# Fewer v transfers, a shorter weight conversion and a zero-padded v operand in a windowed-attention and FFN kernel

## The chip, the cores and the metric

The kernel runs on one core of a Trainium2 chip. The metric is the device time of one execution in microseconds. Five engines work side by side, each through its own list of instructions in order: PE multiplies matrices (its weight loads are shown as PEld), DVE (VectorE) and ACT (ScalarE) work element by element, POOL (GpSimd) does fills and some elementwise work, and SP issues the transfers between main memory (HBM) and on-chip memory (SBUF). PE writes its results to PSUM, from where DVE and ACT read them.

## The reference

Attention over a causal window of 64 positions for 8 batches of 8 heads (576 positions, head dimension 64), and a two-layer FFN with softplus on the result (4608 tokens, 512 to 2048 to 512):

```python
scores = scale * np.matmul(q, k.transpose(0, 1, 3, 2))
mask = (rel >= 0) & (rel < 64)
scores = np.where(mask, scores, -1000000000.0)
scores = scores - np.max(scores, axis=-1, keepdims=True)
attn = np.exp(scores)
attn = attn / (np.sum(attn, axis=-1, keepdims=True) + 1e-09)
attn_out = np.matmul(attn, v).astype(np.float32)
x = attn_out.transpose(0, 2, 1, 3).reshape(B * S, H * D)
h = x @ w_in
g = np.maximum(h, 0.0) + np.log1p(np.exp(-np.abs(h)))
out = (g @ w_out).astype(np.float32)
```

q, k and v are float32, the two weight matrices float64.

## The kernel before, in words

The 4608 tokens are cut into 12 blocks of 384 (three tiles of 128). A block is worked on by head pairs: four pairs `hp`, each of two heads `hh`. The result of a pair is a tile x of 128 rows (features) by 384 tokens; four of them make the x of a block. In the profile's names x_3_0 is pair 3 of the first block, x_3_1 pair 3 of the second. x is kept as a high and a low part in a reduced f32 format, and so are the weights, so that each FFN product is made of three passes (high by high, high by low, low by high).

**FFN.** `ffn_up(g, f)` takes block g and slice f of 16 of the hidden layer: twelve passes on PE into `ps_h` (L403), three ACT steps and two DVE steps for the softplus and the split of g. `ffn_down(g, f)` is nine passes on PE into three banks `ps_o` (L424) that stay open over all slices. The first block is run for slices 0 to 7, the second for all 16, then the first for 8 to 15, then the other ten blocks.

**Weights.** They lie in HBM as float64 bits. `load_w(f)` loads slice f of both matrices (`raws`; later slices in two halves, `raw`) and makes float32 of it from the two 32-bit words of each number: ACT takes the absolute value of the high word read as a float32 (L167), four DVE steps put exponent, sign and mantissa together (L168 to L171), then ACT copies out the high part (L174) and POOL subtracts for the low part (L175). There are 20 such tiles: 12 with both matrices (`ws`, 1024 elements a row) and 8 with one (`wh`, 512).

**Attention of the first two blocks** (`by_pe`). q and k are used as they are: one product per tile into PSUM (L255), DVE adds the mask and finds the extreme of each row (L266), ACT takes the exponential (L276), DVE normalizes (L281 to L284), PE transposes (L291), and L349 multiplies with v in f32. For that product v lies in `v_pad` in two layouts that are shifted by 64 rows. Each head has 128 columns there, its own 64 and 64 zeros, so that both heads of a pair sum into one PSUM tile of 128 rows. The zeros come from two DVE memsets at the start (L121); the loads go tile by tile, nine for a pair (L226, L230).

**Attention of the other ten blocks.** q and k are split into a high and a low part (L237 to L244) and multiplied at L259. The normalized scores P and v are split in three bf16 parts. P goes through two transposing transfers (`nat` to `tr`); `v12` holds parts 1 and 2 of v side by side, so 128 columns of weights for a head, and `v13` holds part 3 of v in its lower half of rows and part 1 in its upper half, 64 columns for a head. The result is summed over up to seven pieces of the window with v12 (PSUM rows 0 to 127) and as many with v13 (PSUM rows 0 to 63), all at L378; then the two halves of the PSUM tile are added (L383, L384).

**Order.** The program makes a list of events with due times (`CONVERT`, `BASE`, `PACE`, `STG0` and so on) and emits them by due time. For events due before 100 (`PE_ORDERED_FROM`) the framework's scheduler sets the order of all engines from its own estimates of durations, so an edit moves instructions that it does not touch. From 100 on PE keeps the order in which the program emits, and the scheduler orders the others. SP has one queue for all transfers and issues them in its list's order; a transfer whose buffer is not free holds those behind it.

Of the kernel before, what the change touches and what calls it, by code (L numbers as in the profile page):

```python
# [20 lines left out]
CH = 64  # L21
NCH = TB // CH + 1
# [9 lines left out]
PE_ORDERED_FROM = 100  # L32
MANUAL = {mybir.EngineType.PE}

ZERO_HIGH = 2.0**-15


@with_exitstack
def window_attention_softplus_ffn(
# [24 lines left out]
    nc = tc.nc  # L64
# [44 lines left out]

    kbd_s = [att.tile([P, 2, CH + TB], F32, name="kbd", tag=f"k{i}") for i in range(2)]
    for t in kbd_s:
        nc.gpsimd.memset(t[D:P, 0, :], 0.0)
        nc.gpsimd.memset(t[0:D, 1, :], 0.0)
        nc.gpsimd.memset(t[0:D, 0, 0:CH], 0.0)
        nc.gpsimd.memset(t[D:P, 1, 0:CH], 0.0)
    v_pads = [att.tile([P, 2, NJ, 2, P], F32, name="v_pad", tag=n) for n in ("nat", "tr")]
    for t in v_pads:  # L120
        nc.vector.memset(t, 0.0)  # L121

# [18 lines left out]
    mask_b = cpool.tile([P, W], BF16, name="mask_b")  # L141
    nc.gpsimd.tensor_copy(mask_b, mask)
    nc.gpsimd.memset(mask_b[CH:P, 0:P], FAR)

    mm, tp = nc.tensor.matmul, nc.tensor.transpose

    def load_w(f):


        if f < NE + 4:  # L150
            k = (0, 4, 2, 6)[f % 4] if f < NE else (4, 6)[f % 2]
            parts = [(spare(k, [P, 2, DM], w_words.dtype, "raws"), spare(k + 1, [P, 2, DM], F32, "ws"), 0, 2)]
        else:
            parts = [
                (
                    ff.tile([P, 1, DM], w_words.dtype, name="raw"),
                    att.tile([P, 1, DM], F32, name="wh", tag=("v_in", "v12")[m]),
                    m, m + 1,
                )
                for m in range(2)  # L160
            ]
        for raw, w, m0, m1 in parts:
            nc.sync.dma_start(raw, w_words[f][:, m0:m1, :])
            words = raw.bitcast(U32).rearrange("p m (n two) -> p two m n", two=2)
            low, high = words[:, 0, :, :], words[:, 1, :, :]
            wb = w.bitcast(U32)
            nc.scalar.activation(w, high.bitcast(F32), AF.Abs)  # L167
            nc.vector.tensor_scalar(w, w, ZERO_HIGH, None, ALU.max)  # L168
            nc.vector.tensor_scalar(wb, wb, 3, 0x3FFFFFF8, ALU.logical_shift_left, ALU.bitwise_and)  # L169
            nc.vector.scalar_tensor_tensor(wb, high, 0xC0000000, wb, ALU.bitwise_and, ALU.bitwise_or)  # L170
            nc.vector.scalar_tensor_tensor(wb, low, 29, wb, ALU.logical_shift_right, ALU.bitwise_or)  # L171
# [9 lines left out]
    def attention(g, hp):  # L181
        c0 = hp * P
        t0 = ORDER[g] * TB
# [11 lines left out]
        heads = [slice(0, D), slice(D, P)]  # L195
# [20 lines left out]
        yield  # L216

        if by_pe:
            v_pad = v_pads[hp % 2]

            def load_v(rows, lay, j0, start):
                n = rows.stop - rows.start
                for j in range(j0, NJ):
                    dst = v_pad[rows, lay, j, :, :].rearrange("p h (i d) -> p (h i) d", i=2)[:, 0:4:3, :]
                    s = start + j * P
                    nc.sync.dma_start(dst, v[s : s + n, c0 : c0 + P].rearrange("p (h d) -> p h d", h=2))  # L226

            if t0 == 0:
                dst = v_pad[CH:P, 0, 0, :, :].rearrange("p h (i d) -> p (h i) d", i=2)[:, 0:4:3, :]
                nc.sync.dma_start(dst, v[0:CH, c0 : c0 + P].rearrange("p (h d) -> p h d", h=2))  # L230
            load_v(slice(0, P), 0, 1 if t0 == 0 else 0, t0 - CH)
            load_v(slice(0, CH), 1, 0, t0 + CH)
            load_v(slice(CH, P), 1, 0, t0)
# [16 lines left out]
        for j in range(NJ):  # L250
# [5 lines left out]
            else:  # L256
                for hh in range(2):
                    for i, part in enumerate((k_hi, k_lo)):
                        mm(  # L259
                            spv[:, hh, :], q_hl[:, hh, js], part[:, hh, kc],  # L260
                            start=(hh == 0 and i == 0), stop=(hh == 1 and i == 1), skip_group_check=True,
                        )
            t = ORDER[g] * NJ + j
# [9 lines left out]
        for hh in range(2):  # L273
            for j in range(NJ):
                i = hh * NJ + j
# [9 lines left out]
        if by_pe:  # L285

            pt = att.tile([P, 2, TB], F32, name="pt", tag="q_hl")
# [5 lines left out]
        else:  # L293

            nat = att.tile([P, 2, 4 * NJ, 2, CH], BF16, name="nat")
            tr = att.tile([P, 8 * NJ, P], BF16, name="tr")
# [5 lines left out]
            n = 4 * NJ  # L302
# [17 lines left out]
            yield  # L320

            v12 = att.tile([P, NCH, 2, 2, D], BF16, name="v12")
            v13 = att.tile([P, NCH, 2, D], BF16, name="v13")
            vv = v_in.rearrange("p c (h d) -> p c h d", h=2)
            up, low = heads
            nc.scalar.copy(v12[:, :, :, 0, :], vv)  # L326
            nc.vector.tensor_tensor(vv, vv, v12[:, :, :, 0, :], ALU.subtract)  # L327
            yield
            nc.scalar.copy(v12[:, :, :, 1, :], vv)
            nc.vector.tensor_tensor(v13[low, :, :, :], vv[low, :, :, :], v12[low, :, :, 1, :], ALU.subtract)  # L330
            nc.vector.tensor_copy(v13[up, :, :, :], v12[up, :, :, 0, :])
        yield

        if hp == 0:
# [5 lines left out]
        if by_pe:  # L340
            av = bank()
# [3 lines left out]
        for hh in range(2):  # L345
            if by_pe:
                for a in range(2 * NJ):
                    cs = slice(a * CH, (a + 1) * CH)
                    mm(  # L349
                        av[:, cs], v_pad[:, a % 2, a // 2, hh, :], pt[:, hh, cs],  # L350
                        start=(hh == 0 and a == 0), stop=(hh == 1 and a == 2 * NJ - 1), skip_group_check=True,
                    )
                if hh == 1:
                    nc.scalar.copy(x_t[0], av[:, :TB])
                    nc.vector.tensor_tensor(x_t[1], av[:, :TB], x_t[0].bitcast(F32), ALU.subtract)
                yield
                continue
            av = bank()
            passes = []
            for s in range(2):  # L360
                for c in range(0 if prev else 1, NCH):


                    j = (c - 1) // 2
                    n = s * 4 * NJ + (hh * NJ + j) * 2
# [10 lines left out]
                    passes.append((s, c, src, slice(o, o + (CH if c in (0, NCH - 1) else P))))  # L376
            for i, (s, c, src, osl) in enumerate(passes):
                mm(  # L378
                    av[: D if s else P, osl], v13[:, c, hh, :] if s else v12[:, c, hh, :, :], src,
                    start=(i == 0), stop=(i == len(passes) - 1), skip_group_check=True,  # L380
                )
            ds = heads[hh]
# [142 lines left out]
```

## Time and profile before

| | |
|---|---|
| three runs | 1057.53, 1059.34 and 1063.11 us, median 1059.34 |
| the profiled execution | 1059.67 us, of it span 1057.9 us |
| mean granted PE clock | 0.977 |
| busy in the span | PE 1004.5, PEld 883.0, DVE 813.9, ACT 740.2, POOL 54.4 us |
| DMA | 119.06 MB, mean 113 GB/s |
| L403 (up), L424 (down), PE busy | 448.9 and 436.4 us |
| L378, L259, L349, PE busy | 78.8, 78.8 and 25.8 us |

Busy time of PE is the union of its instructions, whose ends are modelled; how dense PE really is, is read from the distance between the starts of neighbouring instructions. A share of busy time is a mean over stages, so it is read by stretch. In the timeline a row merges neighbouring instructions of one line and shows the shape of the first; in the rows of groups the figures are the count, then busy us and mean ns of one, then idle us of the engine before them and who ended that.

### The profile page before, as it was taken

The numbers are of one execution on the slowest core, as the hardware profiler recorded it, in microseconds if no ns is written. First come the engines' busy times: TensorE is split into PE (matmuls) and PEld (weight loads), VectorE is DVE, ScalarE is ACT, GpSimd is POOL, SyncE is SP. The second block draws the span as 40 slices with busy tenths as digits, with TensorE's granted clock in tenths as the row PEclk, the third lists the DMA queues.
The fourth block names the chain that finished last, engine by engine and source line by source line (L and its number), as shares of the span: only waits on it lengthen the run. The fifth ranks groups of instructions, "written<-read, shape, count | busy, mean of one in ns | idle before, by whom it ended". The sixth has DMA issues, their size and how long they took to land.

```text
span 1057.9 us, 16725 instructions
## 1 busy us (share of the span) xinstructions
PE 1004.5 (95%) x5888; PEld 883.0 (83%) x5888; DVE 813.9 (77%) x1797; ACT 740.2 (70%) x1705; POOL 54.4 (5%) x53
## 2 busy tenths in 40 slices
PE   5768589999989999999999999999999999999998
PEld 3657488888778988888888888888888888888997
DVE  7889989667986778878877877877887887875322
ACT  4566479677776678778868877877877877865443
POOL 3233420000000000000000000000000000000000
PEclk8989769999999999999999999999999999999999
DMA  6576246344653436635534534534544554631000
GB/s 199 164 260 192 71 137 154 86 128 92 155 116 80 110 80 113 158 80 111 159 81 110 156 84 110 145 95 101 144 105 94 144 112 85 145 57 30 30 1 30
DMA packets 209748, 119.06 MB, mean 113 GB/s; under 512 B 143360, under 2 KB 201728, under 8 KB 208128
## 3 DMA queue, kind: packets, MB, share of 16 engines
q1 hardware_dynamic: 209664, 118.00, 45.0%
q8 instruction: 46, 0.75, 0.3%
q14 instruction: 38, 0.31, 0.1%
HBM read 76.28 MB, written 10.22 MB: 82 GB/s over the span
## 4 chain that ended last, share of the span: by engine, by line
PE 83%; DVE 10%; DMA 4%; ACT 1%; issue 1%; SPq 1%; ACTq 0%
PE ps_h L403 35%; PE ps_o L424 35%; PE ps_a L378 6%; PE ps_a L259 6%; DVE st L266 1%; DMA raws<-in_w_words_dram 1%; DVE ws L171 1%; DVE ws L170 1%; DVE st L284 1%; DMA v_in<-in_v_dram 1%; DVE ws L169 1%; DMA tr<-nat 1%; DMA kbd<-in_kT_dram 1%; DMA raw<-in_w_words_dram 1%; DVE ws L168 1%
## 5 line engine op out<-in xcount | busy, mean ns | idle before, releaser
L403 PE MATMUL ps_h<-x,w 128*128 128x384 f32 x2304 | 448.9, 342 | 9.4 <-DVE u L411 8.3
L424 PE MATMUL ps_o<-w,g 128*128 128x512 f32 x1728 | 436.4, 395 | 2.1 <-ACT g L413 2.1
L403 PEld LDWEIGHTS ps_h<-x,w 128*128 128x128 f32 x2304 | 406.8, 190 | 25.6 <-DVE u L411 11.0
L424 PEld LDWEIGHTS ps_o<-w,g 128*128 128x128 f32 x1728 | 319.2, 189 | 60.9 <-ACT g L413 2.7
L407 ACT ACTIVATE u<-ps_h 128x384 f32<-128x384 f32 x192 | 93.9, 489 | 135.3 <-PE ps_h L403 128.5
L411 DVE SCALAR_TENSOR_TENSOR u<-ps_h,u 128x384 f32<-128x384 f32 x192 | 106.2, 554 | 76.5 <-ACT u L409 75.3
L276 ACT ACTIVATE st<-st,mn 128x128 f32<-128x128 f32 x288 | 112.0, 390 | 17.7 <-DVE st L272 17.7
L414 DVE TENSOR_TENSOR g<-u,g 128x384 fp32r<-128x384 f32 x192 | 106.9, 558 | 12.0 <-ACT g L413 10.6
L266 DVE CUSTOM_DVE_ANT_0 st<-ps_a,mask 128x192 f32<-128x192 f32 x216 | 69.7, 352 | 58.5 <-PE ps_a L259 57.1
L408 ACT ACTIVATE u<-u 128x384 f32<-128x384 f32 x192 | 100.7, 526 | 3.3
L409 ACT ACTIVATE u<-u 128x384 f32<-128x384 f32 x192 | 100.3, 522 | 3.8
L378 PEld LDWEIGHTS <-v 128*128 128x128 bf16 (+1 forms) x1088 | 60.3, 104 | 30.8 <-issue 23.3
L378 PE MATMUL ps_a<-tr,v 128*64 128x128 bf16 (+3 forms) x1088 | 78.8, 215 | 3.3 <-DMA tr<-nat 3.3
L259 PE MATMUL ps_a<-k,q_hl 128*128 128x192 f32 x480 | 78.8, 288 | 0.0
L259 PEld LDWEIGHTS ps_a<-k,q_hl 128*128 128x128 f32 x480 | 67.2, 193 | 7.6
L413 ACT CAST g<-u 128x384 fp32r<-128x384 f32 x112 | 57.0, 509 | 21.6 <-DVE u L411 21.2
L307 ACT CAST nat<-st 128x768 bf16<-128x768 f32 x40 | 33.2, 831 | 38.3 <-DVE st L305 38.2
L383 ACT COPY xf<-ps_a 64x384 f32<-64x384 f32 x80 | 38.1, 476 | 25.6 <-PE ps_a L378 24.4
L276 ACT ACTIVATION_READ_ACCUMULATOR st<-st,mn 128x1 f32 x288 | 54.0, 188 | 0.0
L284 DVE TENSOR_TENSOR st<-st,sm 128x768 f32<-128x768 f32 x48 | 50.4, 1049 | 1.2
L384 DVE TENSOR_TENSOR xf<-ps_a,xf 64x384 f32<-64x384 f32 x80 | 43.8, 548 | 6.1 <-ACT xf L383 4.8
L327 DVE TENSOR_TENSOR v_in<-v_in,v 128x896 f32<-128x896 f32 x40 | 43.5, 1087 | 4.5 <-ACT v L326 4.5
(81 smaller groups left out, 885.7 us busy)
## 6 DMA issues: line engine op xcount, KB each, us to landing
k_in<-in_kT_dram SPq DMA_DIRECT2D x80, 224.0 KB, 3.8
v_in<-in_v_dram SPq DMA_DIRECT2D x80, 224.0 KB, 3.6
q_in<-in_qT_dram SPq DMA_DIRECT2D x84, 192.0 KB, 4.0
raws<-in_w_words_dram SPq DMA_DIRECT2D x12, 1024.0 KB, 5.7
out_dram<-raw SPq DMA_DIRECT2D x12, 512.0 KB, 2.8
raw<-in_w_words_dram SPq DMA_DIRECT2D x8, 512.0 KB, 5.3
out_dram<-raw SPq DMA_DIRECT2D x12, 256.0 KB, 2.6
v_pad<-in_v_dram SPq DMA_DIRECT2D x52, 32.0 KB, 2.7
```

The costliest lines, as they stand in the source:

```text
L259: mm(spv[:, hh, :], q_hl[:, hh, js], part[:, hh, kc], start=(hh == 0 and i == 0), stop=(hh == 1 and i == 1), skip_group_check=True,)
L266: nc.vector.tensor_tensor_reduce(st[:, hh, j, :], spv[:, hh, :], m, QSCALE, 3.0e38, ALU.add, ALU.min, mn[:, hh, j : j + 1])
L276: nc.scalar.activation(sv[:, i, 0:P], sv[:, i, 0:P], AF.Exp, bias=mn[:, hh, j : j + 1], scale=-1.0, accum_out=sm[:, i : i + 1])
L284: nc.vector.tensor_tensor(pn, pn, sm.unsqueeze(2).to_broadcast([P, 2 * NJ, P]), ALU.mult)
L378: mm(av[: D if s else P, osl], v13[:, c, hh, :] if s else v12[:, c, hh, :, :], src, start=(i == 0), stop=(i == len(passes) - 1), skip_grou ...
L403: mm(hv, weight(0, a, f)[:, c * P : (c + 1) * P], x[b][c], start=(i_mm == 0), stop=(i_mm == 3 * NC - 1))
L407: nc.scalar.activation(u, hv, AF.Abs)
L408: nc.scalar.activation(u, u, AF.Exp, scale=-1.0)
L409: nc.scalar.activation(u, u, AF.Ln, bias=1.0)
L411: nc.vector.scalar_tensor_tensor(gf, hv, 0.0, u, ALU.max, ALU.add)
L414: nc.vector.tensor_tensor(gt[1], gf, gt[0].bitcast(F32), ALU.subtract)
L424: mm(ops[g][j], gt[a][:, js], weight(1, b, f), start=(first and i == 0), stop=(last and i == 2),)
```

## The change

Three edits.

1. `v_pad` with its zeros is gone. `v_t` holds the pair's 128 columns without padding, and L347 writes each head's result into its own half of the PSUM rows with 64 columns of weights. All tiles of a layout come in one transfer: four loads for a pair of the first block, three for the second. Only a piece of 64 by 128 of each `v_t` is zeroed, by POOL.
2. The weights' ACT step scales by 2 to the power of -112, so that the exponent is right after the shift by 3 bits. The step that raised small values (L168) is gone; the sign step takes one bit in place of two.
3. `v13` becomes one tile for the whole program with 64 zero columns beside each head's 64, zeroed once by POOL. Its passes use 128 columns of weights and write all 128 PSUM rows.

```diff
-ZERO_HIGH = 2.0**-15
+REBIAS = 2.0**-112
...
-    v_pads = [att.tile([P, 2, NJ, 2, P], F32, name="v_pad", tag=n) for n in ("nat", "tr")]
-    for t in v_pads:
-        nc.vector.memset(t, 0.0)
+    v13 = cpool.tile([P, NCH, 2, 2, D], BF16, name="v13")
+    v_ts = [att.tile([P, 2, NJ, P], F32, name="v_t", tag=n) for n in ("nat", "tr")]
+    for t in v_ts:
+        nc.gpsimd.memset(t[0:CH, 0, 0, :], 0.0)
...
+    nc.gpsimd.memset(v13, 0.0)
...
-            nc.scalar.activation(w, high.bitcast(F32), AF.Abs)
-            nc.vector.tensor_scalar(w, w, ZERO_HIGH, None, ALU.max)
-            nc.vector.tensor_scalar(wb, wb, 3, 0x3FFFFFF8, ALU.logical_shift_left, ALU.bitwise_and)
-            nc.vector.scalar_tensor_tensor(wb, high, 0xC0000000, wb, ALU.bitwise_and, ALU.bitwise_or)
+            nc.scalar.activation(w, high.bitcast(F32), AF.Abs, scale=REBIAS)
+            nc.vector.tensor_scalar(wb, wb, 3, None, ALU.logical_shift_left)
+            nc.vector.scalar_tensor_tensor(wb, high, 0x80000000, wb, ALU.bitwise_and, ALU.bitwise_or)
             nc.vector.scalar_tensor_tensor(wb, low, 29, wb, ALU.logical_shift_right, ALU.bitwise_or)
...
-            def load_v(rows, lay, j0, start):
+            def load_v(rows, lay, j0, j1, start):
                 n = rows.stop - rows.start
-                for j in range(j0, NJ):
-                    dst = v_pad[rows, lay, j, :, :].rearrange("p h (i d) -> p (h i) d", i=2)[:, 0:4:3, :]
-                    s = start + j * P
-                    nc.sync.dma_start(dst, v[s : s + n, c0 : c0 + P].rearrange("p (h d) -> p h d", h=2))
+                src = v[start + j0 * P : start + j1 * P, c0 : c0 + P].rearrange("(j p) n -> p j n", p=P)
+                nc.sync.dma_start(v_t[rows, lay, j0:j1, :], src[:n, :, :])
...
-            nc.vector.tensor_tensor(v13[low, :, :, :], vv[low, :, :, :], v12[low, :, :, 1, :], ALU.subtract)
-            nc.vector.tensor_copy(v13[up, :, :, :], v12[up, :, :, 0, :])
+            nc.vector.tensor_tensor(v13[low, :, :, 0, :], vv[low, :, :, :], v12[low, :, :, 1, :], ALU.subtract)
+            nc.vector.tensor_copy(v13[up, :, :, 0, :], v12[up, :, :, 0, :])
...
-                        av[:, cs], v_pad[:, a % 2, a // 2, hh, :], pt[:, hh, cs],
-                        start=(hh == 0 and a == 0), stop=(hh == 1 and a == 2 * NJ - 1), skip_group_check=True,
+                        av[heads[hh], cs], v_t[:, a % 2, a // 2, heads[hh]], pt[:, hh, cs],
+                        start=(a == 0), stop=(a == 2 * NJ - 1), skip_group_check=True,
...
-                    av[: D if s else P, osl], v13[:, c, hh, :] if s else v12[:, c, hh, :, :], src,
+                    av[:, osl], (v13 if s else v12)[:, c, hh, :, :], src,
```

The new listing is two lines shorter: L403 is now L401, L424 is L422, L378 is L376, L349 is L347, L259 is L258, L291 is L290, and the DVE steps of the conversion are L171 to L173.

What the scheduler makes of it at three places. First SP, from behind the first pair's q and k: the loads of the first block. Before:

```order
3 L163 DMA raws<-in_w_words_dram 128x1024
4 L230 DMA v_pad<-in_v_dram 64x2x64
5 L226 DMA v_pad<-in_v_dram 128x2x64 x2
6 L226 DMA v_pad<-in_v_dram 64x2x64 x6
7 L202 DMA q_in<-in_qT_dram 128x384
8 L204 DMA kbd<-in_kT_dram 64x384 x2
```

And now, from the second pair's v to that of the third:

```order
12 L226 DMA v_t<-in_v_dram 64x3x128 x2
13 L204 DMA k_in<-in_qT_dram 128x384
14 L206 DMA kbd<-in_kT_dram 64x384 x2
15 L166 DMA raws<-in_w_words_dram 128x1024
16 L204 DMA q_in<-in_qT_dram 128x384
17 L206 DMA kbd<-in_kT_dram 64x384 x2
18 L166 DMA raws<-in_w_words_dram 128x1024 x2
19 L166 DMA raw<-in_w_words_dram 128x512 x2
20 L166 DMA raws<-in_w_words_dram 128x1024 x2
21 L229 DMA v_t<-in_v_dram 64x128
```

Before, each pair's loads and one slice of weights took turns; now weights (raws, raw) stand ahead of the third pair's v.

Second DVE, ahead of the last pair of the first block (x_3_0 is its result; sm and st are the softmax). Before:

```order
99 L284 TENSOR_TENSOR st<-st,sm 128x6x128
100 L272 TENSOR_TENSOR st<-st 128x6x64
101 L292 COPY pt<-ps_o_412 128x384
102 L281 TENSOR_SCALAR sm<-sm 128x6
103 L282 RECIPROCAL sm<-sm 128x6
104 L284 TENSOR_TENSOR st<-st,sm 128x6x128
105 L355 TENSOR_TENSOR x_3_0_418<-ps_o_419,x_3_0_417 128x384
```

Now, a little ahead of x_2_0 and x_3_0:

```order
89 L171 TENSOR_SCALAR ws<-ws 128x1024
90 L173 SCALAR_TENSOR_TENSOR ws<-raws,ws 128x1024
91 L283 TENSOR_TENSOR st<-st,sm 128x6x128
92 L172 SCALAR_TENSOR_TENSOR ws<-raws,ws 128x1024
93 L280 TENSOR_SCALAR sm<-sm 128x6
94 L173 SCALAR_TENSOR_TENSOR ws<-raws,ws 128x1024
95 L281 RECIPROCAL sm<-sm 128x6
96 L291 COPY pt<-ps_a 128x384
97 L283 TENSOR_TENSOR st<-st,sm 128x6x128
98 L171 TENSOR_SCALAR ws<-ws 128x1024
```

Conversion steps now stand between the softmax steps. Counted up to x_3_0 there were four of each of L168 to L171 on `ws` (and the two memsets); now there are 10 of L171 and 9 each of L172 and L173 on `ws`, and two each on `wh`. The softmax group of the second block's first pair, which stood ahead of x_3_0, now stands behind it. Counted up to x_3_1 there were 12 tiles of `ws` and 5 of `wh` (each of four steps); now 12 of `ws` and 6, 5 and 5 steps on `wh`.

Third PE, a head of a later block: the last v12 pass, the v13 passes and what follows. Before:

```order
3151 L378 MATMUL ps_a<-tr,v_5661 128x64
3152 L378 LDWEIGHTS v_5662
3153 L378 MATMUL ps_a<-tr,v_5662 64x128
...
3163 L378 MATMUL ps_a<-tr,v_5662 64x64
3164 L259 MATMUL ps_a<-k_5642,q_hl 128x192
```

Now:

```order
3192 L376 MATMUL ps_a<-tr,v_5581 128x64
3193 L376 LDWEIGHTS v_99
3194 L376 MATMUL ps_a<-tr,v_99 128x128
...
3204 L376 MATMUL ps_a<-tr,v_99 128x64
3205 L258 MATMUL ps_a<-k_5562,q_hl 128x192
```

The order there is the same; the v13 passes write 128 rows (the first figure) where they wrote 64, and v_99 is the one v13 of the whole program. On POOL the fill of v13 (128x1792) stands between the fills of the mask and the steps that finish it.

More of the change, by code (lines that the diff above doesn't have):

```diff
@@ L218, in attention @@
         if by_pe:
-            v_pad = v_pads[hp % 2]
-            def load_v(rows, lay, j0, start):
+            v_t = v_ts[hp % 2]
+            def load_v(rows, lay, j0, j1, start):
                 n = rows.stop - rows.start
-                for j in range(j0, NJ):
-                    dst = v_pad[rows, lay, j, :, :].rearrange("p h (i d) -> p (h i) d", i=2)[:, 0:4:3, :]
-                    s = start + j * P
-                    nc.sync.dma_start(dst, v[s : s + n, c0 : c0 + P].rearrange("p (h d) -> p h d", h=2))
+                src = v[start + j0 * P : start + j1 * P, c0 : c0 + P].rearrange("(j p) n -> p j n", p=P)
+                nc.sync.dma_start(v_t[rows, lay, j0:j1, :], src[:n, :, :])
             if t0 == 0:
[L229 to L233, printed above, removed]
+                nc.sync.dma_start(v_t[CH:P, 0, 0, :], v[0:CH, c0 : c0 + P])
+            load_v(slice(0, P), 0, 1 if t0 == 0 else 0, NJ, t0 - CH)
+            load_v(slice(0, CH), 1, 0, NJ, t0 + CH)
+            load_v(slice(CH, P), 1, 0, NJ, t0)
         else:
@@ L322, in attention @@
             v12 = att.tile([P, NCH, 2, 2, D], BF16, name="v12")
-            v13 = att.tile([P, NCH, 2, D], BF16, name="v13")
             vv = v_in.rearrange("p c (h d) -> p c h d", h=2)
```

## The prediction

> **What bounds the kernel now.** I read the page's busy shares, its forty slices and its chain of waits first, to see which engine sets the end and whether it is the same everywhere.
>
> ```profile
> PE 1004.5 (95%) x5888; PEld 883.0 (83%) x5888; DVE 813.9 (77%) x1797; ACT 740.2 (70%) x1705; POOL 54.4 (5%) x53
> ...
> PE   5768589999989999999999999999999999999998
> ...
> DVE  7889989667986778878877877877887887875322
> ...
> PE 83%; DVE 10%; DMA 4%; ACT 1%; issue 1%; SPq 1%; ACTq 0%
> ```
>
> PE holds 83% of the chain, but in the first six slices (26 us each) it has holes while DVE stands at 7 to 9 tenths. So there are stages with different limits, and I cut the span with the table of windows (stretch, length, busy us and instructions of PE, PEld, DVE, ACT and POOL, then granted clock, DMA share, GB/s).
>
> ```profile
> 0.00:51.90 51.90, 33.44 (x174) 24.30 (x175) 41.15 (x106) 25.82 (x82) 15.49 (x29) 0.93 0.63 177
> 51.90:136.00 84.10, 62.19 (x302) 53.16 (x300) 76.22 (x126) 48.50 (x111) 32.70 (x20) 0.83 0.53 173
> ...
> 160.00:320.00 160.00, 154.42 (x942) 133.99 (x941) 126.03 (x281) 122.32 (x285) 0.00 (x0) 1.00 0.51 121
> 320.00:1000.00 680.00, 680.00 (x4116) 604.26 (x4115) 531.06 (x1196) 502.07 (x1145) 0.00 (x0) 1.00 0.45 106
> ```
>
> From 320 to 1000 us PE has no idle time and DVE is busy 531 of 680 us: there PE's pitch counts and DVE's work does not. From 51.9 to 136 us it is the other way round: DVE is busy 76.2 of 84.1 us, PE 62.2. The third view is the timeline of the start (start, length, engine, line; in brackets the wait before it).
>
> ```profile
> 30.49 2.89 PE L349 MATMUL ps_o<-pt,v_pad 128*128 128x64 f32 x24 [0.55 <-ACT pt L292]
> ...
> 51.32 0.56 DVE L355 TENSOR_TENSOR x<-ps_o,x 128x384 fp32r<-128x384 f32 x1
> ...
> 129.02 1.51 PE L291 MATMUL ps_a<-ident,st 128*128 128x128 f32 x6 [10.77 <-DVE st L284]
> 130.46 5.38 PE L349 MATMUL ps_a<-pt,v_pad 128*128 128x64 f32 x24
> ```
>
> The L355 row is the last quarter of the first block's x (x_3_0), without which no FFN sum of that block ends; the last two belong to the last quarter of the second block, for which PE stood 10.8 us behind DVE. These two are my marks, at 51.9 and 136 us.
>
> **Part 1, zero columns beside part 3 of v.** Per head PE makes seven passes with 128 columns of weights (v12), then seven with 64 (v13), then goes on to other work. The timeline of PE shows a whole head, and twice a run of seven wide passes alone.
>
> ```profile
> 471.68 0.97 PE L378 MATMUL ps_a<-tr,v 128*128 128x64 bf16 x14
> 472.58 0.36 PE L259 MATMUL ps_a<-k,q_hl 128*128 128x192 f32 x1
> ...
> 288.51 0.51 PE L378 MATMUL ps_a<-tr,v 128*128 128x64 bf16 x7 [0.55 <-DMA tr<-nat]
> 288.86 0.34 PE L259 MATMUL ps_a<-k,q_hl 128*128 128x192 f32 x1
> ...
> 306.65 0.51 PE L378 MATMUL ps_a<-tr,v 128*128 128x64 bf16 x7
> 307.00 0.45 PE L259 MATMUL ps_a<-k,q_hl 128*128 128x192 f32 x2
> ```
>
> From start to start, seven wide passes up to the next L259 take 0.35 us, both times; so fourteen of them should take 0.70. The head as it is takes 0.90 (472.58 less 471.68). The 0.20 us lies in the two changes of width, into the narrow run and out of it, and the change removes both. Where the passes lie:
>
> ```profile
> 160.00:320.00 160.00, 17.05 (x221) 12.35 (x221) 1.00 0.51 121
> 320.00:1000.00 680.00, 61.79 (x867) 47.95 (x867) 1.00 0.45 106
> ```
>
> (PE and PEld on L378 alone.) Of 80 heads (10 blocks, 4 pairs, 2 heads) 867/1088 or 64 lie where PE never idles: 64 x 0.20 = 12.8 us. The 16 others lie where PE is busy 154.4 of 160 us: 3.2 x 0.965 = 3.1. Sum: **-15.9 us**. Bounds: -8 if only one of the two changes goes away, 0 if the wide runs were short for another reason. I take the full one, since both lone runs give the same figure. The writes of v13 now land in pieces of 64: even at twice the time their cover is the 149 us that DVE idles from 320 to 1000 us, and without that cover PE would wait the same time.
>
> **Part 2, three steps instead of four.** The groups of DVE from 0 to 136 us (line, tile, count, busy us, mean ns, idle before):
>
> ```profile
> L171 DVE SCALAR_TENSOR_TENSOR ws<-raws,ws 128x1024 uint32<-128x1024 uint32 x12 | 16.9, 1406 | 0.1
> L170 DVE SCALAR_TENSOR_TENSOR ws<-raws,ws 128x1024 uint32<-128x1024 uint32 x12 | 15.5, 1291 | 0.1
> L284 DVE TENSOR_TENSOR st<-st,sm 128x768 f32<-128x768 f32 x8 | 12.1, 1510 | 0.0
> L169 DVE TENSOR_SCALAR ws<-ws 128x1024 uint32<-128x1024 uint32 x12 | 9.3, 772 | 0.0
> L168 DVE TENSOR_SCALAR ws<-ws 128x1024 f32<-128x1024 f32 x12 | 8.9, 739 | 6.0 <-ACT ws L167 6.0
> ...
> L170 DVE SCALAR_TENSOR_TENSOR wh<-raw,wh 128x512 uint32<-128x512 uint32 x5 | 5.5, 1094 | 0.1
> ...
> L171 DVE SCALAR_TENSOR_TENSOR wh<-raw,wh 128x512 uint32<-128x512 uint32 x5 | 4.2, 846 | 0.1
> L169 DVE TENSOR_SCALAR wh<-wh 128x512 uint32<-128x512 uint32 x5 | 4.1, 822 | 0.1
> L168 DVE TENSOR_SCALAR wh<-wh 128x512 f32<-128x512 f32 x5 | 3.4, 680 | 2.6 <-ACT wh L167 2.6
> ```
>
> Gone is L168: 8.9 + 3.4 = 12.3 us of the stage in which DVE is the limit. The other three keep kind and shape, so I keep their prices (the shift alone could be a little below 772 ns; not counted).
>
> But DVE's order changes too. Ahead of x_3_0 there were 4 tiles of four steps: 4 x (0.739 + 0.772 + 1.291 + 1.406) = 16.8 us. Now there are 10 + 9 + 9 steps on ws and 2 of each on wh: 7.7 + 24.3 + 5.5 = 37.5. Gone from there are the two memsets (2.7 us, which lay in DVE's first idle time) and one softmax group of the second block (L284 at 1.5 and three small ones, about 2.5). So x_3_0 has 20.7 - 2.7 - 2.5 = 15.5 us more ahead of it: 41.15 + 15.5 = 56.7 us of work, plus idle time. That was 51.9 - 41.15 = 10.75, and most of it must stay, for the chain of waits has this row at its start:
>
> ```profile
> 2.45 6.73 DMA raws<-in_w_words_dram
> ```
>
> The first weights land at 9.2 us and DVE has little to do before. With 8 to 10.75 idle, x_3_0 falls at 65 to 67; I take 66 us: **14 us later than now**.
>
> From there to the second mark the conversions were 8 x 4.21 + 5 x 3.44 = 50.9 of the 76.2 us; 25.3 were other work. Now they are 1.5 + 8.1 on ws and 3.3 + 5.8 on wh, 18.7, and with the softmax group 46.5 us. At the share now seen (76.2/84.1 = 0.91) that is 51 us: second mark at 117, a gain of 19. If PE sets the pace instead, its 62.2 us remain: mark at 128, a gain of 8. I take the middle, **-13 us**. Ends: -25 if DVE never waits behind the first weights (65 + 46.5 = 111), +14 if the second stretch still takes its 84 us.
>
> On that PE pace the clock bears:
>
> ```profile
> 120.00:130.00 10.00, 0.98 (x5) 1.01 (x6) 9.06 (x13) 5.42 (x19) 5.65 (x5) 0.55 0.15 54
> 130.00:140.00 10.00, 9.43 (x41) 8.81 (x40) 6.64 (x11) 5.30 (x10) 2.80 (x2) 0.50 0.57 187
> ```
>
> Behind the 10.8 us wait the granted clock is 0.50, and the same 24 passes of L349 take 5.38 us, not 2.89. The Trainium skill (TensorE: Matmul & The Clock Gate, part 1 on the HAM clock gate) says that the clock halves after an idle window of about 3.4 us; the row agrees. If that wait falls under this, those passes alone give 2.5 us more, and the sum would be 1028.
>
> **Part 3, v in fewer transfers.** The block by PE issues 28 v loads, not 72. The SP queue's rows and POOL's fills:
>
> ```profile
> 3.77 6.67 SPq L226 DMA_DIRECT2D v_pad<-in_v_dram  x8
> ...
> L127 POOL MEMSET mask<- 128x192 bf16 x1 | 0.3, 268 | 0.1
> ```
>
> At 6.67/8 = 0.83 us, 44 issues are 37 us of the queue: weights are asked for sooner, which is the idle time already counted above, and no more, since DVE then has enough of them. L349 now loads 64 columns: its price lies between the present one and half of it, 1.4 us less for each of the four groups in the second stretch; 0 to 6 us of PE time, inside the spread between 8 and 19. POOL fills v13 ahead of the mask: at most 1792/192 x 0.27 = 2.5 us, and the first softmax may start that much later; it is covered by DVE's idle time before the first weights land, and uncovered it would cost the 2.5. Taken as 0.
>
> **Sum.** Profiled execution 1059.67 us (span 1057.9 and 1.8 around it): 1059.7 - 15.9 - 13 = 1030.8, so **1031 us**. The median of the runs shown is 0.3 us off that, which I leave.
>
> **Rivals.**
> *The start gives nothing back.* x_3_0 comes 14 us late, and FFN steps of ACT, DVE and PE that follow each other keep either engine from its pace, so the second stretch shrinks by just 14. For: four raws and two raw loads in a row now stand ahead of the third pair's v in SP's queue, and hold it until DVE has freed their buffers. Against: DVE's 30 us less. 1059.7 - 15.9 = 1044.
> *The width is not what costs.* The narrow runs' 0.20 us goes to something else that stays. For: no run here has fourteen wide passes. Against: the two lone runs. 1059.7 - 13 = 1047.
> *The start is bound by DVE alone,* and its waits for weights vanish: 1059.7 - 15.9 - 25 = 1019.
> *Slower: the padded loads are dear.*
>
> ```profile
> L259 PEld LDWEIGHTS ps_a<-k,q_hl 128*128 128x128 f32 x480 | 67.2, 193 | 7.6
> L378 PEld LDWEIGHTS <-v 128*64 128x64 bf16 x544 | 31.3, 110 | 13.3 <-issue 7.3 <-DVE sm L281 0.4
> L378 PEld LDWEIGHTS <-v 128*128 128x128 bf16 x544 | 29.0, 98 | 17.5 <-issue 15.9 <-DMA tr<-nat 1.2 <-ACT u L409 0.3
> ```
>
> Were a wide load of v13 paced like the f32 one, 193 ns instead of 98, PE would lose 95 ns on each of 544: +51.7, or 1082. It decides from (28.9 + 5.3)/544 = 63 ns a load on. Against: v12's wide bf16 loads take 98 ns, less than the narrow ones' 110. The Trainium skill (same page, "LDWEIGHTS (loading the stationary operand)") gives columns/1.2 ns, so 53 ns more for 64 columns more: an estimate of +29 us and 1060; the section on weight-path perf modes there exempts 128 columns that are not fp32, and the two rows side with it.
>
> **How the numbers follow.** Forecast 60%, no gain at the start 17%, DVE alone 12%, width 8%, dear loads 3%. The range, 1016 to 1047, holds all but the dear loads, the far end of the late start (up to 1058) and part of the width case. About 0.5%, 5 us, is what a measurement can tell from no change: faster 0.94; same 0.03 (the late start's far end); slower 0.03 (the dear loads).
>
> **What would show it.** Right: a head's fourteen passes to the next L258 in 0.70 us; the 680 us stretch some 13 shorter; x_3_0 near 66 us and the last L290 of the second block without a 10 us wait. Wrong: fourteen passes still at 0.90, PEld on v13 near 193 ns, x_3_1 at 136 us or behind it, or new PE waits from 320 us on.

## The result, and the profile after

The changed kernel takes 1032.08 us (median of 4 runs, 1030.02 to 1033.06), beside 1059.82 us of the kernel before on the same chip (4 runs, 1057.53 to 1063.11). The ratio is 0.9733, 95% interval 0.9703 to 0.9764: 2.7% faster, 28 us. The prediction was 1031. The profiled execution took 1030.02 us, of it span 1028.2.

The same views as in the prediction, now of the kernel after. First the page's busy shares and the forty slices (25.7 us each).

```profile
PE 974.8 (95%) x5888; PEld 859.1 (84%) x5888; DVE 802.6 (78%) x1775; ACT 742.0 (72%) x1705; POOL 61.8 (6%) x56
...
PE   4559889999999999999999999999999999999998
...
DVE  6998587797987888878878878878878887874332
```

PE has become worse in the first three slices, not better (4, 5, 5 against 5, 7, 6); it is better in the next two (9 and 8 against 8 and 5) and full from the seventh on (before, the twelfth still had 8). The table of windows says the same by stage (stretch, length, then busy us and instructions of PE, PEld, DVE, ACT, POOL, granted clock, DMA share, GB/s).

```profile
0.00:51.90 51.90, 24.27 (x96) 14.20 (x96) 42.66 (x89) 25.25 (x62) 23.98 (x34) 0.75 0.79 262
51.90:136.00 84.10, 65.12 (x381) 51.72 (x382) 64.97 (x128) 50.85 (x134) 30.95 (x18) 0.89 0.40 127
136.00:160.00 24.00, 22.12 (x112) 19.25 (x111) 23.69 (x54) 20.63 (x46) 6.84 (x4) 0.95 0.60 142
160.00:320.00 160.00, 159.57 (x986) 140.85 (x987) 127.12 (x283) 124.83 (x288) 0.00 (x0) 1.00 0.50 116
320.00:1000.00 680.00, 680.00 (x4204) 612.41 (x4202) 536.46 (x1210) 510.55 (x1158) 0.00 (x0) 1.00 0.44 106
```

Up to 51.9 us PE does 96 instructions where it did 174. From 160 to 320 us it stands still for 0.43 us, where it stood 5.58. From 320 us on it is full, as before. The row of the third stretch in the kernel before, for the clock:

```profile
136.00:160.00 24.00, 20.80 (x95) 19.44 (x96) 21.96 (x56) 19.26 (x43) 6.17 (x4) 0.74 0.47 136
```

The timeline shows the marks and a head of the steady part (start, length, engine, line; in brackets the wait ahead). First PE and DVE at the start, then two heads.

```profile
55.68 1.51 PE L290 MATMUL ps_a<-ident,st 128*128 128x128 f32 x6 [10.62 <-DVE st L283]
...
69.56 0.54 DVE L353 TENSOR_TENSOR x<-ps_o,x 128x384 fp32r<-128x384 f32 x1
...
128.61 1.51 PE L290 MATMUL ps_a<-ident,st 128*128 128x128 f32 x6 [2.76 <-DVE st L283]
...
134.94 0.56 DVE L353 TENSOR_TENSOR x<-ps_a,x 128x384 fp32r<-128x384 f32 x1
```

```profile
473.65 0.85 PE L376 MATMUL ps_a<-tr,v 128*128 128x64 bf16 x14
474.33 0.67 PE L258 MATMUL ps_a<-k,q_hl 128*128 128x192 f32 x4
...
476.95 0.85 PE L376 MATMUL ps_a<-tr,v 128*128 128x64 bf16 x14
477.64 0.67 PE L258 MATMUL ps_a<-k,q_hl 128*128 128x192 f32 x4
```

x_3_0 comes at 70.1 us (51.9 before). The 10.8 us wait ahead of the second block's last transposes has shrunk to 2.76, but a wait of 10.62 us now stands in the first block. x_3_1 comes at 135.5 (137.0 before, by the same row). Fourteen passes now take 0.68 and 0.69 us to the next L258.

The FFN's 4032 matmuls come block by block and slice by slice in every kernel here, so the start of the n-th of them (counted from 0) says about how far a kernel is; the table gives it for before, and the difference to before for the change and, ahead of the experiments, for four of them (us; minus is earlier).

| n | before at | after | part 1 alone | part 2 alone | part 3 alone | parts 1 and 2 |
|---|---|---|---|---|---|---|
| 24 (first of the third slice) | 62.1 | +19.9 | -1.4 | -0.3 | +21.8 | -1.7 |
| 186 (at the second mark) | 136.4 | -1.5 | -0.9 | -11.1 | +5.4 | -11.5 |
| 300 | 171.3 | -5.3 | -0.1 | -10.9 | +4.9 | -11.8 |
| 1000 | 345.9 | -16.1 | -3.5 | -17.3 | +4.6 | -23.8 |
| 4031 (last) | 1053.3 | -29.9 | -18.6 | -15.6 | +6.3 | -37.6 |

In the change only 1.5 us are won at the second mark, 14.6 between there and 346 us, and 13.8 behind it.

### The profile page after: what moved, and what is told of

The parts are those of the page before. It is cut to its first block, busy times and chain, and to the rows that moved or that the text cites. A ratio compares the mean times of both kernels' runs of the same rounds, so it can differ in the third digit from the quotient of the medians.

```text
span 1028.2 us, 16614 instructions
## 1 busy us (share of the span) xinstructions
PE 974.8 (95%) x5888; PEld 859.1 (84%) x5888; DVE 802.6 (78%) x1775; ACT 742.0 (72%) x1705; POOL 61.8 (6%) x56
## 4 chain that ended last, share of the span: by engine, by line
PE 85%; DVE 9%; DMA 2%; ACT 1%; issue 1%; SPq 1%; DVEq 0%; ACTq 0%
PE ps_o L422 37%; PE ps_h L401 37%; PE ps_a L376 5%; PE ps_a L258 5%; DVE ws L172 2%; DVE ws L173 1%; DVE st L265 1%; DVE st L283 1%; DMA raws<-in_w_words_dram 1%; DVE ws L171 1%; DVE st L271 0%; DMA tr<-nat 0%; ACT st L275 0%; PE ps_a L254 0%; DVE sm L280 0%
## 5 line engine op out<-in xcount | busy, mean ns | idle before, releaser
L401 PE MATMUL ps_h<-x,w 128*128 128x384 f32 x2304 | 445.3, 340 | 7.6 <-ACT x L352 3.9
L422 PE MATMUL ps_o<-w,g 128*128 128x512 f32 x1728 | 435.5, 395 | 0.0
L401 PEld LDWEIGHTS ps_h<-x,w 128*128 128x128 f32 x2304 | 402.6, 189 | 22.5 <-ACT x L352 5.2
L422 PEld LDWEIGHTS ps_o<-w,g 128*128 128x128 f32 x1728 | 318.0, 188 | 57.7 <-ACT g L411 0.3
L258 PE MATMUL ps_a<-k,q_hl 128*128 128x192 f32 x480 | 76.5, 283 | 0.0
L376 PEld LDWEIGHTS <-v 128*128 128x128 bf16 x1088 | 56.1, 98 | 22.9 <-issue 21.8
L376 PE MATMUL ps_a<-tr,v 128*128 128x128 bf16 (+1 forms) x1088 | 72.0, 213 | 0.2
L258 PEld LDWEIGHTS ps_a<-k,q_hl 128*128 128x128 f32 x480 | 66.6, 192 | 4.1 <-issue 0.5
L283 DVE TENSOR_TENSOR st<-st,sm 128x768 f32<-128x768 f32 x48 | 47.6, 991 | 1.5
```

Source lines behind the costliest of these rows:

```text
L258: mm(spv[:, hh, :], q_hl[:, hh, js], part[:, hh, kc], start=(hh == 0 and i == 0), stop=(hh == 1 and i == 1), skip_group_check=True,)
L283: nc.vector.tensor_tensor(pn, pn, sm.unsqueeze(2).to_broadcast([P, 2 * NJ, P]), ALU.mult)
L376: mm(av[:, osl], (v13 if s else v12)[:, c, hh, :, :], src, start=(i == 0), stop=(i == len(passes) - 1), skip_group_check=True,)
L401: mm(hv, weight(0, a, f)[:, c * P : (c + 1) * P], x[b][c], start=(i_mm == 0), stop=(i_mm == 3 * NC - 1))
L422: mm(ops[g][j], gt[a][:, js], weight(1, b, f), start=(first and i == 0), stop=(last and i == 2),)
```

## The experiments

**Each part alone, and the first two together.** Part 1 alone is the kernel before with

```diff
-                    av[: D if s else P, osl], v13[:, c, hh, :] if s else v12[:, c, hh, :, :], src,
+                    av[:, osl], (v13 if s else v12)[:, c, hh, :, :], src,
```

and its wide, once zeroed `v13`; part 2 alone is the four lines of `load_w`; part 3 alone is `v_t` with its merged loads and 64-column products.

> The kernel before, with part 1 of the change alone: v13 as one tile with zero columns, 128 columns of weights in its passes. Theory (a change of weight width costs PE 0.1 us each time, and PE has no idle time from 320 us on): 0.20 us for each of 80 heads less, so 1059.8 - 16 = 1044 us; seven v13 passes after seven v12 passes and on to L259 in about 0.70 us, no gap of 0.12 us at the change. The order of DVE and SP at the start stays that of the kernel before, so the mark x_3_1 stays near 136 us. Rival (the 0.20 us belongs to something else): 1060 us.

> The kernel before, with part 2 alone: weight conversion in three DVE steps. The scheduler keeps the order of before here: 12 conversion steps ahead of x_3_0 where there were 16 (4 tiles both times), 47 ahead of x_3_1 where there were 68. Theory (DVE sets the pace from 52 to 136 us, and an own order is what kept the whole change from gaining there): mark x_3_1 about 12 us sooner, near 124 us, total 1059.8 - 12 = 1048 us. Rival (removed steps come back as longer ones beside POOL, and PE or ACT sets the pace): mark within 4 us of 136, total 1056 us or more.

> The kernel before, with part 3 alone: v in fewer transfers, no padding, 64 columns of weights at L347. The scheduler puts 45 conversion steps (four to a tile) ahead of x_3_0 here, where there were 16. Theory (this part is what moves conversions ahead and delays the first block's x): x_3_0 not at 52 but near 85 us (29 steps of about 1.05 us more), and since the conversions are then done early, the mark x_3_1 moves less, to 136 to 146 us; total 1060 to 1070 us, no gain. Rival (fewer transfers help by themselves): total 1050 us.

> Parts 1 and 2 without part 3: v_pad with its nine loads and DVE's memsets stays. Order of the start as before, with three steps to a tile. Theory (the parts add, and part 3 costs by the order that it brings): 1059.8 - 16 - 12 = 1032 us or a little less, level with or below the full change's 1032. Rival (part 3's shorter queue is what gave the start its gain): 1040 us or more.

| kernel | median us | ratio to before, 95% |
|---|---|---|
| part 1 alone | 1041.49 | 0.9809 (0.9779 to 0.984) |
| part 2 alone | 1041.93 | 0.9823 (0.9801 to 0.9846) |
| part 3 alone | 1065.99 | 1.0041 (1.0024 to 1.0058) |
| parts 1 and 2 | 1020.42 | 0.9616 (0.9594 to 0.9638) |
| all three | 1032.08 | 0.9733 (0.9703 to 0.9764) |

Of 1060 us these are -20, -19, +4, -41 and -28. Parts 1 and 2 add up (39 against 41). Against the expectations, part 1 came out 2.5 us better, part 2 6 us better, and both together 12 us better than the 1032 that I had; part 3 fell within its range, with x_3_0 at 75.5 us instead of near 85. Part 3 costs 4 us by itself and about 12 on top of the other two. So the change holds a faster kernel, that without its third part.

Part 2 alone, windows: with the fourth step gone and v loaded as before, PE has no idle time left from 160 us on (154.42 of 160 before).

```profile
51.90:136.00 84.10, 69.72 (x360) 60.37 (x361) 71.85 (x135) 56.48 (x135) 31.44 (x20) 0.86 0.57 186
160.00:320.00 160.00, 160.00 (x973) 139.37 (x972) 125.39 (x270) 122.81 (x277) 0.62 (x1) 1.00 0.46 113
```

**Is it the change of width that costs?** The same passes, but sorted so that v12 and v13 take turns, in the kernel before and in the kernel after:

```diff
+            passes.sort(key=lambda e: (e[1], e[0]))
```

> The kernel before with the passes of a head in another order: v12 and v13 of the same piece of the window one after the other, so weights of 128 and 64 columns alternate: 13 changes of width inside a head where there was 1. Theory (a change of width costs about 0.09 us more than the 0.056 us pitch): 12 x 0.09 = 1.1 us a head, 64 heads where PE never idles: 70 us, and up to 86 with the others: 1130 to 1146 us. Rival (the cost belongs to the start and end of a head): 1060 us.

> The full change with the same alternating order of passes; here all weights have 128 columns. Theory (only a change of width costs): no difference, 1032 us within 4. Rival (alternating between the two v tiles costs by itself, whatever their width): as much more as in the narrow case.

With the narrow v13 the kernel takes 1160.53 us, 100 more; with the wide one 1030.9, no difference to 1032.08 that one run could tell (each of the two is a single run). The expectation of 1130 to 1146 was too low, since it had 0.09 us for a change. The timeline of PE, narrow and taking turns:

```profile
506.61 2.31 PE L379 MATMUL ps_a<-tr,v 128*128 128x64 bf16 x14
508.85 0.69 PE L259 MATMUL ps_a<-k,q_hl 128*128 128x192 f32 x4
...
511.49 2.31 PE L379 MATMUL ps_a<-tr,v 128*128 128x64 bf16 x14
513.73 0.69 PE L259 MATMUL ps_a<-k,q_hl 128*128 128x192 f32 x4
```

A head takes 2.24 us with fourteen changes (the last into L259), 0.90 with two, 0.68 with none: (2.24 - 0.68)/14 = 0.11 us for a change, and (0.90 - 0.68)/2 = 0.11 as well. The price is for the change, not for the columns. Single instructions show both ways: in the narrow run that takes turns, the starts of passes lie 160 and 176 ns apart in turn, and 56 ns apart where all are wide.

**What in part 3 costs?** My first theory was the order alone. By the program's own lists, so many conversion steps stand on DVE ahead of the x of each pair (steps of all kinds, three to a tile with part 2; the column of x_2_1 is counted in the traces, which give the same counts for the others):

| kernel | ahead of x_3_0 | x_0_1 | x_1_1 | x_2_1 | x_3_1 | median us |
|---|---|---|---|---|---|---|
| parts 1 and 2 | 12 | 14 | 29 | 37 | 47 | 1020.42 |
| full change | 34 | 40 | 48 | 48 | 52 | 1032.08 |
| full, weights held | 14 | 29 | 38 | 46 | 50 | 1042.35 |
| full, one transfer a slice | 12 | 13 | 26 | 37 | 48 | 1022.08 |
| one transfer a slice, early weights | 32 | 38 | 48 | 48 | 49 | 1028.27 |
| full, merged in three late pairs only | 12 | 13 | 28 | 43 | 48 | 1026.64 |
| full, 128-row slices merged only | 12 | 15 | 36 | 44 | 48 | 1029.14 |
| full, 64-row slices merged only | 34 | 40 | 48 | 48 | 50 | 1038.45 |

The first try held the loads of eight weight slices back by force, with a copy of one element from an x into the buffer that the load is to fill:

```diff
+            hold = {4: 2, 5: 2, 6: 3, 7: 3, 12: 3, 13: 3, 14: 3, 15: 3}.get(f)
+            if hold is not None:
+                nc.vector.tensor_copy(raw.bitcast(F32)[0:1, 0, 0:1], xs[0][0][hold][0:1, 0:1].bitcast(F32))
```

> The full change, and in front of the loads of weight slices 4 to 7 and 12 to 15 one DVE copy of a single element of the first block's x (pair 2 or 3) into the tile that is loaded, so that these loads cannot start before that x is there; nothing else is touched. Conversion steps ahead of x_3_0: 14, where the full change has 34 and parts 1 and 2 without part 3 have 12. Theory (part 3 costs by the order alone, conversions ahead of the first block's x): x_3_0 near 50 us instead of 69, the mark x_3_1 at 122 to 126 instead of 135, total 1015 to 1023 us. Rival (the new v tiles, their transfers or the narrow weights of L347 cost by themselves): 1030 us or more although the order is held.

1042.35 us, ratio 0.9846 (0.9811 to 0.9882): 10 us slower than the full change. x_3_0 did come early, at 57.6 us, but what was held back then fell due in one lump, 29 steps ahead of x_0_1 where parts 1 and 2 have 14; x_0_1 came at 81.6 us against 63.7. PE was busy only 153.03 of the 160 us from 160 us on. The theory in that form fell: an early x_3_0 is not enough.

The second try undoes one thing in the full change, the merging of the transfers. A pair has nine v loads again, 72 in all (the 18 a pair in the expectation is a slip); tiles, products and fills stay as in the change.

```diff
-                src = v[start + j0 * P : start + j1 * P, c0 : c0 + P].rearrange("(j p) n -> p j n", p=P)
-                nc.sync.dma_start(v_t[rows, lay, j0:j1, :], src[:n, :, :])
+                for j in range(j0, j1):
+                    s = start + j * P
+                    nc.sync.dma_start(v_t[rows, lay, j, :], v[s : s + n, c0 : c0 + P])
```

> The full change with one thing undone: the 128-column v tiles (no padding, 64-column loads on the twelve-pass and the part-3 lines as in the full change) are fetched with one transfer for each 128-row slice, 18 a pair, instead of three or four merged ones. By the program, twelve conversion steps then stand ahead of x_3_0 on VectorE and 13 ahead of x_0_1, as without part 3 (12 and 14), against 34 and 40 in the full change. Theory (it is the shorter queue of SP, through the order of the conversions, that costs; the tiles without padding cost nothing): time 1015 to 1022 us, x_3_0 at 52 to 57 us, FFN at the second mark 10 us or more ahead of before. Rival (the unpadded tiles, the narrow loads or the fills on GpSimd cost by themselves): 1028 us or more, about as the full change, with x_3_0 at 65 us or later.

1022.08 us (5 runs, 1020.35 to 1025.55), ratio 0.9637 (0.9617 to 0.9656): about 10 us faster than the full change. So the unpadded tiles, the narrow products and POOL's fills cost nothing that shows; the merging, with what it brings, does. Its window around the first mark, and below it that of the full change:

```profile
30.00:70.00 40.00, 32.07 (x197) 24.27 (x198) 31.12 (x77) 25.00 (x79) 7.97 (x5) 0.87 0.55 172
```

```profile
30.00:70.00 40.00, 20.68 (x120) 13.22 (x118) 40.00 (x75) 22.27 (x52) 22.86 (x13) 0.74 0.62 200
```

In the full change DVE works without a gap for these 40 us, PE does 120 instructions instead of 197, and at a clock of 0.74 instead of 0.87. x_3_0 comes at 52.3 us here, at 70.1 there.

The medians differ by 10.0 us, but these two profiled executions by only 4.5 (1025.55 the slowest of its five, 1030.02 the fastest of its four). What follows on part 3 therefore goes by medians and intervals.

The third try asks for the order without the merging: the kernel just shown, with one line changed.

```diff
-CONVERT = (-104, -98, -93, -88, -6, -3, 0, 3, 6, 8, 11, 13, 16, 18, 21, 24)
+CONVERT = (-104, -102, -97, -93, -92, -91, -90, -89, -85, -84, -6, -3, 16, 18, 21, 24)
```

> No transfer is merged (nine v loads a pair, 72 in all, as in the run of 1022 us); in its place the table of the weight conversions asks for slices 1 to 11 earlier (-102 to -84 and -6, -3 in place of -98 to 13), so that by the program the conversions stand ahead of the x's nearly as in the full change: 9, 12, 28, 32 steps ahead of x_0_0 to x_3_0, 38 ahead of x_0_1, 48 ahead of x_1_1 (full change 13, 16, 32, 34, 40, 48). Theory (the order costs, not the merging): 1028 to 1038 us, x_3_0 at 64 us or later. Rival (merging costs by itself): 1020 to 1026 us.

1028.27 us (5 runs, 1027.83 to 1029.28), ratio 0.9708 (0.9694 to 0.9722), 6.2 us slower than with the weights in their old place, with no transfer merged. Its window, and x_3_0 on the timeline of DVE:

```profile
30.00:70.00 40.00, 23.92 (x126) 16.59 (x124) 39.74 (x71) 22.14 (x58) 18.78 (x12) 0.67 0.70 231
```

```profile
68.05 0.56 DVE L354 TENSOR_TENSOR x<-ps_o,x 128x384 fp32r<-128x384 f32 x1
```

That is the picture of the full change: DVE full, PE at 126 instructions, x_3_0 at 68.6. So weights and conversions that are put ahead of the first block's x cost about 6 us by themselves.

The other side, merging with the order as good as it can be kept, was tried three ways: merged only in the last three pairs of the second block (`t0 > 0 and hp >= 1`), only for the slices of 128 rows (`lay == 0`), and only for those of 64 (`lay == 1`). By the traces these have 54, 60 and 40 v loads; the 56 and 48 in the expectations of the last two are slips.

> The full change with the merging kept only for the last three pairs of the second block (54 v loads), where it leaves the conversions nearly as they stand with one transfer a slice: 12 steps ahead of x_3_0, 13 ahead of x_0_1, 28 ahead of x_1_1. Theory (merging costs through the order that it brings): 1019 to 1026 us, as with one transfer a slice (1022). Rival (a merged transfer costs by itself, about 10 us for eight pairs): 3 to 4 us more for three pairs, 1025 to 1027 us, or more if the late pairs are the ones that matter.

> The full change with the merging kept only for the slices of 128 partitions (one transfer of two or three slices for each pair) and the 64-partition slices fetched one by one again: 56 v loads in all, not 28. By the program 12 conversion steps stand ahead of x_3_0 and 15 ahead of x_0_1, and 36 ahead of x_1_1. Theory (merging costs only through the order of the conversions that it brings): 1018 to 1026 us, x_3_0 at 52 to 58 us. Rival (a merged transfer costs by itself, by landing later or by the traffic it brings): half of the 10 us or more of the full change against one transfer a slice, 1026 us or more.

> The other half: the merging kept only for the slices of 64 partitions (two transfers of three slices a pair), the 128-partition slices fetched one by one: 48 v loads in all. By the program 34 conversion steps stand ahead of x_3_0 and 40 ahead of x_0_1, as in the full change. Theory (the order is what costs): 1028 to 1036 us, about as the full change, x_3_0 at 66 to 72 us. Rival (a merged transfer costs by itself): a part of the cost only, 1024 to 1028 us, near the other half's time.

| merged | median us | ratio to before, 95% | x_3_0 at |
|---|---|---|---|
| nothing | 1022.08 | 0.9637 (0.9617 to 0.9656) | 52.3 |
| three late pairs | 1026.64 | 0.9685 (0.9668 to 0.9701) | 50.9 |
| 128-row slices | 1029.14 | 0.9702 (0.9684 to 0.9719) | 49.5 |
| 64-row slices | 1038.45 | 0.979 (0.976 to 0.982) | 72.2 |
| all | 1032.08 | 0.9733 (0.9703 to 0.9764) | 70.1 |

The half that I expected at 1018 to 1026 came at 1029.14 and the late pairs just above the theory's 1026, both where the rival had them (1026 or more, 1025 to 1027); the half of 1028 to 1036 came at 1038.45, outside both ranges. In each, x_3_0 came where the number of steps ahead of it said; the end came later than that. Two things follow. A fixed price for a merged transfer is excluded: merging the 128-row slices costs 7 us where nothing else is merged, and saves 6 where the 64-row slices are merged already. And the steps ahead of x_3_0 alone do not set the time either: with 12 the times go from 1020 to 1029, with 34 from 1032 to 1038. In the run with the 128-row slices merged, 36 steps stand ahead of x_1_1 where 26 did, so its loss may still be order, later on. In the run with the late pairs it is 28 there, but 43 ahead of x_2_1 where the unmerged kernel has 37, and that x comes at 116.9 us instead of 107.2; so its 4.6 us may be order as well. Sorted by the steps ahead of x_2_1 the medians run 1020 and 1022 (37), 1027 (43), 1029 (44), 1028 to 1038 (48); only the kernel with the weights held (46 steps, 1042) falls out of line. No run varies that count alone.

Wherever the loss is, it lies early: from the 1000th FFN matmul to the last, each kernel of the table of steps except that one gains 13.8 or 13.9 us on the kernel before. The profile of the late pairs has one wait of 3.8 us in that early time, from 160 to 320 us (PE behind ACT's L446), that the unmerged kernel's profile does not have; whether merging brings it, no run shows. That part is open.

## Why the prediction was right, and where it was not

**Part 1 (-15.9): right in mechanism, 2 to 4 us too small.** The passes take 0.68 instead of 0.90, 0.22 a head where I had 0.20: 80 x 0.22 = 17.6. Part 1 alone is 18.6 us earlier at the last FFN matmul of its profile, 15.1 of it behind 346 us. The rival that something else in the narrow runs costs is excluded by the two runs that take turns: 100 us with twelve more changes in each of 64 heads and ten more in the 16 that have twelve passes (100/928 = 0.11 us each), nothing where all passes are wide.

**Dear padded loads: excluded.** All loads of L376 are of one form now.

```profile
L376 PEld LDWEIGHTS <-v x1088: 95/98/102, 164.7 to 946.1; 128*128 128x128 bf16 x182
```

The median is 98 ns, as for v12 before. The Trainium skill's price by columns (TensorE: Matmul & The Clock Gate, "LDWEIGHTS (loading the stationary operand)") would have made them 53 ns dearer than the narrow ones, by the estimate in the prediction; its section on weight-path perf modes exempted them, and the trace agrees with that one.

**First mark: 70.1 instead of 66.** DVE did 60.9 us of work up to it, not 56.7, while its idle time, 9.2 us, lay where I had it (8 to 10.75): the steps that remain have become longer on average. DVE's groups from 0 to 136 us (busy, mean ns, idle before):

```profile
L172 DVE SCALAR_TENSOR_TENSOR ws<-raws,ws 128x1024 uint32<-128x1024 uint32 x12 | 20.0, 1666 | 0.0
L173 DVE SCALAR_TENSOR_TENSOR ws<-raws,ws 128x1024 uint32<-128x1024 uint32 x12 | 16.1, 1338 | 0.0
L171 DVE TENSOR_SCALAR ws<-ws 128x1024 uint32<-128x1024 uint32 x12 | 11.9, 995 | 1.6 <-ACT ws L170 1.6
```

The step of 1291 ns takes 1666 and that of 772 takes 995; only the last is shorter (1338 for 1406). Together 48.0 us where the same three took 41.7. Of the 8.9 us that L168 held on `ws`, 6.3 came back. "The other three keep their prices" was wrong for the mean. It holds for a step that runs alone, as the shortest ones show (min, median, max in ns; L170 before, the same step as L172 after):

```profile
L170 DVE SCALAR_TENSOR_TENSOR ws<-raws,ws x12: 1208/1224/2060, 12.3 to 113.4; 128x1024 uint32<-128x1024 uint32 x12
```

```profile
L172 DVE SCALAR_TENSOR_TENSOR ws<-raws,ws x12: 1212/1669/2294, 11.5 to 85.1; 128x1024 uint32<-128x1024 uint32 x12
```

Compared one by one with POOL's instructions, every step on `ws` during which POOL does nothing takes 646 to 695 ns (L171; before, L168 and L169) or 1207 to 1226 (L172 and L173; before, L170 and L171). All longer ones share time with POOL: 6 of 48 before, 14 of 36 now. So the means that I carried over held the share of steps beside POOL, and the new order raised that share. No run takes POOL's work away, so that POOL is the cause is read from the trace and not tested.

**Second mark at 117 to 128: the step that failed.** x_3_1 came at 135.5. DVE's work between the marks was what I counted (46.5), and PE had less than the 62.2 that I gave it:

```profile
70.10:135.50 65.40, 53.27 (x306) 43.31 (x306) 46.27 (x99) 39.60 (x107) 18.10 (x12) 0.92 0.33 104
```

But the stretch took 65.4 us with DVE busy 46.27 (0.71, not the 0.91 that I carried over) and PE 53.27 (0.81). Neither engine was full, so neither set the pace alone. Of PE's 12.1 idle us, 8.3 stand behind the softmax on DVE, and 2.9 behind ACT:

```profile
PE ps_a L290 <- DVE st L283: 8.3, 3, 5.0
PE ps_h L401 <- ACT x L352: 2.9, 1, 2.9
```

The stretch shrank from 84.1 to 65.4, by 18.7, about as much as x_3_0 was late (18.2). At this mark the rival "the start gives nothing back" was right, and not my -13. Part 2 alone, in the order of before, does gain there: x_3_1 comes at 127.4, 9.5 us sooner. The wait ahead of the last transposes did shrink (2.76 us), and the granted clock from 125 to 135 us was 0.82 where it was 0.50; L347's 24 passes took 2.04 us there, but the mark did not move with them.

**Where the 13 us came from instead.** The sum of part 2 and the order did come to about that: 29.9 us at the last FFN matmul less the 17.3 of part 1 (13.8 behind 346 us, 3.5 ahead of it by the run of part 1 alone) is 12.6. But it lies behind the mark: from 136 to 160 us the clock is 0.95 where it was 0.74, and from 160 to 320 us PE's idle 5.58 us are gone. An estimate from the rows of windows: 22.12 x 0.95 less 20.80 x 0.74 is 5.6 us of PE at full clock, and with 5.15 us less idle time that is 10.8 of the 12 us that the change wins between the mark and 346 us apart from part 1. Part 2 alone has a clock of 1.00 in the first of these stretches and no idle time in the second, part 1 alone 0.80 and 6.6 us, part 3 alone 0.68 and 3.4 us, so that gain is part 2's. The number came out right through a gain in a place where I had put none, which stood in for one that did not come. That is luck, as it is that the 41 us of parts 1 and 2 less the 12 that part 3 takes leave the 29 of my sum.

**Part 3 (0): wrong.** I said that the shorter queue only asks for weights sooner, in idle time, "and no more". It puts 34 steps ahead of x_3_0 instead of 12, and on top of parts 1 and 2 it costs about 12 us; I had priced its delay at the first mark but not seen that parts 1 and 2 need not have it. About 6 us are shown to come from early weights alone; the rest is not settled. L347 is cheaper than L349:

```profile
65.51 0.91 PE L347 MATMUL ps_o<-pt,v_t 128*64 128x64 f32 x12
...
67.40 0.91 PE L347 MATMUL ps_o<-pt,v_t 128*64 128x64 f32 x12
```

Two such rows make a group, 1.82 us at full clock where 2.89 stood. That gain does not show in any time: the kernel with wide padded products, 1020.42, is not slower than the one with narrow ones, 1022.08.

## What to carry to other kernels

Where runs of matmuls with wide and narrow weights alternate, as here in bf16 with 128 and 64 columns, try padding the narrow ones with zeros, and count the changes of width, not the columns. Where a scheduler orders the program, treat each edit as an edit of the order: an edit that only shortens a queue can pull later work ahead of what everything waits for, so try each part of a change alone, and the change without each part. And do not carry the busy share of one engine over to a stretch in which its work shrinks: once it is no longer the bound, nothing makes it, or the next engine, keep that share.

## What was not expected of the hardware

A change between 64 and 128 columns of weights cost 0.11 us in these bf16 passes, about 0.10 us into the narrow pass and 0.12 out of it (160 and 176 ns less 56), twice as much as a pass of the wide run (0.68/14 = 0.05). A load of 64 columns took longer than one of 128 (110 against 98 ns). And the DVE step L172 took 1666 ns on average where the same step took 1291 before, with 1208 to 1226 in both kernels for one that runs while POOL does nothing; POOL's L177 took 1768 where it took 1584, in the same stretch:

```profile
L177 POOL TENSOR_TENSOR w<-ws,w 128x512 fp32r<-128x512 f32 x24 | 41.9, 1768 | 42.1 <-ACT w L176 42.1
```

Each DVE step on `ws` that is longer shares time with POOL, which speaks for contention between the two, but no run set them apart.
